# More filler transposes on TensorE in the first six pairs, written into idle columns of the score tile

## The chip, the cores and the metric

The kernel runs on one core of one Trainium2 chip. The metric is the device time of one execution in microseconds. Before the change it is 695.62 us, the median of three runs (695.5 to 698.72).

## What is computed

Attention over 8 batches of 8 heads, 576 positions and 64 features, with rotary positions on q and k, and then a gated feed-forward layer over the 512 features that the eight heads make together. Everything is in 32-bit floats. Cut to what matters:

```
q_rot, k_rot = rotate(q), rotate(k)
scores = q_rot @ k_rot.T / 8
scores = scores - max(scores, axis=-1)
attn = exp(scores);  attn = attn / (sum(attn, axis=-1) + 1e-9)
x = attn @ v                                   # heads side by side: (8, 576, 512)
gate = sigmoid(sum over 5 taps of conv_w[k] * x shifted by 4 - k rows)
out = ((gate * (x @ w_val)) @ w_out)
```

## The kernel before

**Pairs.** Two heads make a pair, so there are 32 pairs, four for each batch. A pair is worked through in five query chunks. Four of them have 128 queries for each of the two heads, the fifth, the odd chunk, holds the last 64 queries of both heads.

**A score step.** `s_mm` (L331) multiplies a chunk's queries with all 576 keys. It writes one score tile per head, two for a full chunk and one for the odd one. A score tile has two banks of PSUM, 2 x 512 columns, of which 2 x 288 are used. VectorE takes the maximum of each row (`s_max`, L337, tile `nm`), ScalarE the exp with the row sums (`s_exp`, L345, tile `p`). There are two score tiles in all (tags `ps_s0` and `ps_s1`), so the next chunk's scores can be written when the exps of this one have ended.

**What follows a step.** TensorE transposes the probabilities (L392, and L357 for the left-over columns) into a bank of another ring of four (tags `ps_t0` to `ps_t3`). ScalarE and VectorE copy them out (L430, L432), and TensorE multiplies them with v (L441, and L451 for the left-over rows) into such a bank. `x_norm` (L492) scales the result with the inverse sums, and the five taps and the gate follow on VectorE and ScalarE (L515 to L523).

**The feed-forward layer.** After every fourth pair, `f_mm` (L558) multiplies a batch's x with the two weights. Its matmuls stand between those of the pairs that follow. Its first ones here belong to batch 0 and stand behind pair 4's scores. Matmul operands are split into a high and a low part, and the weights are unpacked on VectorE (L594 to L606) during the first pairs.

**What sets the order.** A list written out by hand, `ORDER`, names the jobs one by one. Its position in that list is a job's step. Each engine does its jobs in that order. An entry's number after the colon is the ring slot that it takes. The tile framework adds the waits between engines: for every access to a tile it lets the instruction wait for the earlier accesses that it takes to be in conflict with it.

**Fillers.** The table `FILLS` gives some steps a number of transposes of the identity matrix that nobody reads, ahead of the step's job. Before the change there are 92 of them at nine steps, 32 at the very start. Each group takes a whole bank of the `ps_t` ring, whose slot the second number names:

```
def fill(n, slot):
    bank = psum.tile([128, 512], F32, name="ps_t", tag=f"ps_t{slot}")
    for _ in range(n):
        T.transpose(out=bank[:, 0:128], in_=ident, identity=ident)
```

Of the kernel before, what the change touches and what calls it, by code (L numbers as in the profile page):

```python
# [10 lines left out]
F32 = mybir.dt.float32  # L11
# [151 lines left out]
3271 3302:1 3272:1 3303 3273 3304 3274 3298 3305A:0 3299 3306 3312:3 3300A:2 3307:2 3301 3308 3309 3313 3310A:1 3317:1 3311 3318 3314 3319 3315V:0  # L163
3322:0 3320V:2 3323 3321 3324 3316 3325A:1 3326
"""
FILLS = {11: (32, 0), 17: (7, 1), 50: (19, 0), 63: (14, 2), 89: (7, 3), 101: (7, 0), 183: (2, 3), 287: (2, 1), 425: (2, 2)}


class Plan:
# [16 lines left out]
    def run(self, engine, fill):  # L186
# [6 lines left out]
        for step, entry in enumerate(ORDER.split()):  # L193
# [4 lines left out]
            writer.update(dict.fromkeys(w, i))  # L198
            if step in FILLS:
                fill(*FILLS[step])  # L200
            self.slots = [int(x) for x in slots]
# [5 lines left out]
def attn_gated_ffn(ctx: ExitStack, tc: tile.TileContext, q2, k2, v2, tab, w_val, conv_w, w_out, out, collect=None):  # L207
# [14 lines left out]
    V, A, G, T, SP = nc.vector, nc.scalar, nc.gpsimd, nc.tensor, nc.sync  # L222
# [5 lines left out]
    psum = ctx.enter_context(tc.tile_pool(name="psum", bufs=1, space=PSUM))  # L228
# [3 lines left out]
    def ring(tag, shape, dtype, name, where=pool):  # L232

        n = plan.slots.pop(0) if B[tag] > 1 else 0
        return where.tile(shape, dtype, name=name, tag=f"{tag}{n}")

    ident = const.tile([128, 128], F32, name="ident")
# [16 lines left out]
    state = {}  # L254
# [62 lines left out]
    def s_mm(p, c, second):  # L317

        st = state[p]
        heads = (0,) if c == 4 else (0, 1)  # L320
        tiles = []
        for h in heads:
            ps = ring("ps_s", [128, 2, 512], F32, "ps_s", psum)
            st[f"s{2 * c + h}"] = ps[:, :, 0:288]
            tiles.append(ps)
        for half in range(2):
            for i, (x, y) in enumerate(((0, 0), (0, 1), (1, 0))):
                for h in heads:
                    rows = slice(0, 128) if c == 4 else HEAD[h]
                    k0 = (0 if second else D) + half * 288  # L330
                    T.matmul(out=tiles[h][:, half, 0:288], lhsT=st["q"][rows, x, c * 128:c * 128 + 128],  # L331
                             rhs=st["k"][rows, y, k0:k0 + 288], start=(i == 0), stop=(i == 2))
# [14 lines left out]

    def fill(n, slot):

        bank = psum.tile([128, 512], F32, name="ps_t", tag=f"ps_t{slot}")  # L350
        for _ in range(n):
            T.transpose(out=bank[:, 0:128], in_=ident, identity=ident)  # L352

    def transpose(p, key, srcs):
        bank = ring("ps_t", [128, 512], F32, "ps_t", psum)
# [321 lines left out]
    for p in range(NP):  # L677
# [7 lines left out]
        for n in ("k", "q"):  # L685
            cut = 288 if n == "k" else 384
            for a, b in [(0, wide[n])] if p else [(0, cut), (cut, wide[n])]:
# [4 lines left out]
                if p < RAW:  # L692
                    add("GV", rope_mul, p, n, 1, a, b, r=tr + " " + x0, w=x1)
                    add("GV", rope_mul, p, n, 0, a, b, r=tr, w=x0)
                    for i, (x, y) in enumerate(((0, cut), (cut, wide[n]))):
                        if not a <= x < b:
                            continue
                        bank, hi, lo = f"ps_t/{n}{p}.{i}", f"{n}{par}#hi.{i}", f"{n}{par}#lo.{i}"
# [13 lines left out]
        for i, c in enumerate(order(p) + (4,)):  # L712
            r = kr + f" k{par}#w" * (i % 2) + " " + toks(f"q{par}#@.@", ("hi", "lo"), (0,) if c < 3 else R2)
            add("P", s_mm, p, c, i % 2, r=r, w=toks(f"ps_s/{p}.@", (2 * c, 2 * c + 1)[:1 + (c < 4)]))
            for x in (2 * c, 2 * c + 1)[:1 + (c < 4)]:
                t = f"{i // 2}{x % 2}" if c < 4 else "m"
                add("V", s_max, p, x, r=f"ps_s/{p}.{x}", w=f"nm/{p}.{x}")
                add("A", s_exp, p, x, t, i % 2, r=f"ps_s/{p}.{x} nm/{p}.{x}", w=f"p/{p}.{t}#{x} sums{par}#{x}")
# [87 lines left out]
    with tc.manual_schedule():  # L806
        plan.run({"V": V, "A": A, "G": G}, fill)
# [59 lines left out]
```

## Time and profile before

| | |
|---|---|
| runs | 698.72, 695.62, 695.5 us |
| the profiled execution | 699.4 us, span 697.5 us |
| mean granted clock of TensorE | 0.978 of full speed |
| TensorE busy | 669.6 us (96%), 7184 matmuls |
| VectorE busy | 585.9 us (84%) |
| ScalarE busy | 504.4 us (72%) |
| GpSimd busy | 308.1 us (44%) |
| the chain that ended last | TensorE 79%, VectorE 12%, ScalarE 6% |

Times are microseconds from the start of the span, and a matmul's durations overlap with the next one's: a busy TensorE is not TensorE at its peak. PE is TensorE's matmuls, PEld its weight loads, DVE VectorE, ACT ScalarE, POOL GpSimd. A row of the timeline gives the start, the length of the group, the engine, the line, and in brackets how long the engine was idle before it and what ended that. A row of groups gives the count, then busy time and mean ns of one, then the idle time before them and its releasers. A row of windows gives the stretch, and for PE, PEld, DVE, ACT and POOL the busy time with the count of instructions, then the granted clock, the share of the DMA engines and GB/s.

### The profile page before, as it was taken

What the parts mean: (1) busy time and instruction counts of PE and PEld (TensorE: products, weight loads), DVE (VectorE), ACT (ScalarE), POOL (GpSimd) and SP (SyncE); (2) the same over time, 40 slices, a digit from 0 to 9 for tenths busy, and PEclk for the clock granted to TensorE, in tenths of its full rate; (3) what the DMA queues carried; (4) which work ended last, traced back from release to release, by engine and by line L of the source; (5) the groups of instructions that cost most, each with busy time, mean ns of one, the idle gap of its engine ahead of it and who ended that gap; (6) DMA issues with size and microseconds to landing.
All of it is one profiled execution on the core that took longest, in us unless ns stands there. A gap on an engine that the chain in (4) does not pass through costs nothing.

```text
span 697.5 us, 18207 instructions
## 1 busy us (share of the span) xinstructions
PE 669.6 (96%) x7184; PEld 539.9 (77%) x7184; DVE 585.9 (84%) x1012; ACT 504.4 (72%) x1238; POOL 308.1 (44%) x236
## 2 busy tenths in 40 slices
PE   8888899899999999999999999999999999999998
PEld 7656567677778888787878888777788887788887
DVE  5998899999988868989899887998889889787741
ACT  3787877786877887778669877677678786777522
POOL 1344424264354765456334554366445553243031
PEclk9997769999999999999999999999999999999999
DMA  6344332433443143243432152433422144411011
GB/s 222 109 135 142 102 112 75 117 105 103 140 140 105 60 136 121 60 125 112 132 105 82 58 167 78 133 103 114 131 97 65 61 128 123 132 47 35 27 61 68
DMA packets 47318, 72.65 MB, mean 104 GB/s; under 512 B 15961, under 2 KB 25730, under 8 KB 47234
## 3 DMA queue, kind: packets, MB, share of 16 engines
q1 hardware_dynamic: 46690, 70.91, 32.8%
q8 instruction: 56, 0.92, 0.6%
q10 hardware_dynamic: 544, 0.59, 0.3%
q14 instruction: 28, 0.23, 0.1%
HBM read 61.89 MB, written 9.59 MB: 102 GB/s over the span
## 4 chain that ended last, share of the span: by engine, by line
PE 79%; DVE 12%; ACT 6%; issue 3%; POOL 0%; DVEq 0%; ACTq 0%; POOLq 0%
PE ps_f L558 27%; PE ps_s L331 18%; PE ps_a L441 17%; PE ps_t L392 10%; DVE nm L337 4%; ACT p L345 3%; PE ps_a L451 3%; PE ps_t L357 2%; DVE g L518 2%; ACT pt L430 2%; PE ps_t L352 1%; DVE q L303 1%; DVE pt L432 1%; PE ps_r L286 1%; ACT q L295 0%
## 5 line engine op out<-in xcount | busy, mean ns | idle before, releaser
L345 ACT ACTIVATE p<-ps_s,nm 128x576 f32<-128x576 f32 x288 | 212.7, 742 | 70.7 <-DVE nm L337 68.5
L337 DVE TENSOR_REDUCE nm<-ps_s 128x1 f32<-128x576 f32 x288 | 207.9, 750 | 44.7 <-PE ps_s L331 40.4
L331 PE MATMUL ps_s<-k,q 64*128 64x288 f32 (+1 forms) x1728 | 184.4, 315 | 14.6 <-ACT p L345 14.0
L331 PEld LDWEIGHTS ps_s<-k,q 64*128 64x128 f32 (+1 forms) x1728 | 143.6, 190 | 48.0 <-ACT p L345 33.7
L430 ACT COPY pt<-ps_t 128x512 f32<-128x512 f32 (+1 forms) x228 | 120.9, 547 | 54.8 <-PE ps_t L392 52.9
L441 PE MATMUL ps_a<-pt,v 128*64 128x256 f32 (+1 forms) x1024 | 139.9, 416 | 1.2 <-DVE pr L432 0.7
L518 DVE SCALAR_TENSOR_TENSOR g<-x,cw,g 128x576 f32<-128x576 f32 (+1 forms) x132 | 121.0, 918 | 1.4 <-ACT g L515 0.9
L392 PEld LDWEIGHTS ps_t<-ident,p 64*128 64x128 f32 x2428 | 101.5, 141 | 22.4 <-issue 9.6
L392 PE MATMUL ps_t<-ident,p 64*128 64x64 f32 x2428 | 113.4, 229 | 3.9 <-ACT p L345 1.3
L558 PE MATMUL ps_f<-y,wout_hi 128*128 128x288 f32 (+2 forms) x512 | 107.4, 302 | 0.7 <-DVE pt L432 0.5
L441 PEld LDWEIGHTS ps_a<-pt,v 128*64 128x64 f32 x1024 | 68.8, 138 | 46.9 <-issue 3.8
L573 POOL TENSOR_TENSOR y<-y,y 128x288 fp32r<-128x288 f32 (+2 forms) x64 | 57.2, 905 | 105.0 <-ACT y L570 101.6
L558 PEld LDWEIGHTS ps_f<-y,wout_hi 128*128 128x128 f32 x512 | 81.4, 188 | 6.4 <-issue 1.5
L275 POOL TENSOR_TENSOR qin<-qin,tab 128x640 f32<-128x640 f32 (+1 forms) x36 | 58.2, 1627 | 55.1 <-DMA qin<-in_q 44.0
L558 PE MATMUL ps_f<-xh,wval_hi 128*128 128x288 f32 (+2 forms) x256 | 79.1, 313 | 1.1 <-ACT pt L430 1.1
L558 PE MATMUL ps_f<-xh,wval_lo 128*128 128x288 f32 (+2 forms) x256 | 76.4, 301 | 0.0
L558 PE MATMUL ps_f<-xl,wval_hi 128*128 128x288 f32 (+2 forms) x256 | 75.5, 298 | 0.0
L558 PE MATMUL ps_f<-y,wout_lo 128*128 128x288 f32 (+2 forms) x256 | 74.4, 294 | 0.0
L275 POOL TENSOR_TENSOR kin<-kin,tab 128x576 f32<-128x576 f32 x27 | 43.7, 1625 | 62.7 <-DMA kin<-in_k 52.1
L505 POOL TENSOR_TENSOR xl<-x,xh 128x576 fp32r<-128x576 f32 (+2 forms) x33 | 48.2, 1463 | 50.6 <-ACT xh L499 31.1
L432 DVE COPY pt<-ps_t 128x512 f32<-128x512 f32 (+1 forms) x92 | 56.8, 623 | 5.3 <-PE ps_t L392 4.7
L345 ACT ACTIVATION_READ_ACCUMULATOR p<-ps_s,nm 128x1 f32 x288 | 57.3, 199 | 0.0
(87 smaller groups left out, 860.9 us busy)
## 6 DMA issues: line engine op xcount, KB each, us to landing
kin<-in_k SPq DMA_DIRECT2D x31, 576.0 KB
qin<-in_q SPq DMA_DIRECT2D x31, 512.0 KB
v<-in_v SPq DMA_DIRECT2D x32, 320.0 KB
out_t<-o SPq DMA_DIRECT2D x56, 144.0 KB
rb<-rd SPq DMA_DIRECT2D x31, 144.0 KB
rb<-rd SPq DMA_DIRECT2D x31, 128.0 KB
wst<-in_w_val SPq DMA_DIRECT2D x4, 512.0 KB
wst<-in_w_out SPq DMA_DIRECT2D x8, 256.0 KB
```

What stands on the lines that cost most here:

```text
L275: eng.tensor_tensor(out=t[:, i, a:b], in0=t[:, 0 if p < RAW else i, a:b], in1=table[:, i, a:b], op=ALU.mult)
L331: T.matmul(out=tiles[h][:, half, 0:288], lhsT=st["q"][rows, x, c * 128:c * 128 + 128], rhs=st["k"][rows, y, k0:k0 + 288], start=(i == 0), ...
L337: V.tensor_reduce(out=st[f"nm{i}"], in_=st[f"s{i}"], axis=AX.XY, op=ALU.max, negate=True)
L345: A.activation(out=st[f"p{t}"][:, part].rearrange("p (b x) -> p b x", b=2), in_=st[f"s{i}"], func=AF.Exp, bias=st[f"nm{i}"], scale=1.0, ac ...
L392: T.transpose(out=st["b" + key + x][:, k * D:(k + 1) * D], in_=src[rows], identity=ident[rows, rows])
L430: A.copy(out=dst, in_=src)
L432: V.tensor_copy(out=dst, in_=src)
L441: T.matmul(out=st[f"a{g}"][HEAD[h], 0:n], lhsT=st["v"][:, j, h, :], rhs=st[f"pt{g}"][:, h * 4 + j], start=(j == 0), stop=False)
L505: G.tensor_tensor(out=st["xl"][:, a:b], in0=xs[p % 2][:, 4 + a:4 + b], in1=st["xh"][:, a:b].bitcast(F32), op=ALU.subtract)
L518: V.scalar_tensor_tensor(out=g, in0=x_sb[:, a + k:b + k], scalar=w, in1=g, op0=ALU.mult, op1=ALU.add)
L558: T.matmul(out=acc[:, 0:n], lhsT=wt[w][:, kc, ds], rhs=mv, start=(kc == 0 and i == 0), stop=(kc == NCH - 1 and i == 2))
L573: G.tensor_tensor(out=ffn[b][1][:, dc, lo:hi], in0=ffn[b, "y", dc, lo], in1=ffn[b][0][:, dc, lo:hi].bitcast(F32), op=ALU.subtract)
```

## The change

The table has 28 steps in the place of nine, and 242 transposes in the place of 92. The steps lie between 11 and 614 of 3,327, in pairs 0 to 5. All but the two groups at steps 11 and 17 have the slot -1. That sends them to the score tile that was allocated last, into columns 384 to 511 of its second half, which `s_mm` doesn't write. They no longer take a bank of the `ps_t` ring.

```
-FILLS = {11: (32, 0), 17: (7, 1), 50: (19, 0), 63: (14, 2), 89: (7, 3), 101: (7, 0), 183: (2, 3), 287: (2, 1), 425: (2, 2)}
+FILLS = {11: (32, 0), 17: (8, 1), 50: (19, -1), 63: (14, -1), 77: (11, -1), 89: (8, -1), 101: (8, -1), 145: (4, -1), 164: (8, -1), 176: (4, -1), 183: (3, -1),
+         191: (8, -1), 253: (24, -1), 263: (3, -1), 278: (5, -1), 287: (3, -1), 350: (15, -1), 364: (14, -1), 375: (10, -1), 387: (6, -1), 400: (3,
+         -1), 425: (2, -1), 451: (2, -1), 458: (6, -1), 487: (3, -1), 557: (9, -1), 573: (3, -1), 614: (7, -1)}
...
             st[f"s{2 * c + h}"] = ps[:, :, 0:288]
+            state["score"] = ps
...
-        bank = psum.tile([128, 512], F32, name="ps_t", tag=f"ps_t{slot}")
+        if slot < 0:
+            to = state["score"][:, 1, 384:512]
+        else:
+            to = psum.tile([128, 512], F32, name="ps_t", tag=f"ps_t{slot}")[:, 0:128]
         for _ in range(n):
-            T.transpose(out=bank[:, 0:128], in_=ident, identity=ident)
+            T.transpose(out=to, in_=ident, identity=ident)
```

The order on VectorE, ScalarE, GpSimd and the DMA queue is the same as before. TensorE's order differs by the fillers alone. Two places of it follow. In the rows, `[waits ...]` names the engines whose semaphores the instruction waits for, and the six new lines of code move the line numbers: L334 is the old L331, L358 the old L352, L398 the old L392 and L363 the old L357.

TensorE before, pair 0, from the end of the first score step to the transposes behind the second:

```order
L331 MATMUL ps_s<-k_71,q_73 128x288 x7
L352 MATMUL ps_t<-ident 128x128 x19
L331 MATMUL ps_s<-k_71,q_73 128x288 [waits Activation_49] x2
L331 MATMUL ps_s<-k_71,q_73 128x288 x10
L392 MATMUL ps_t<-ident,p 128x64 [waits PE_49]
L392 MATMUL ps_t<-ident,p 128x64 x15
```

The same place after the change:

```order
L334 MATMUL ps_s<-k_71,q_73 128x288 x7
L358 MATMUL ps_s<-ident 128x128 [waits Activation_49]
L358 MATMUL ps_s<-ident 128x128 x18
L334 MATMUL ps_s<-k_71,q_73 128x288 [waits PE_49] x2
L334 MATMUL ps_s<-k_71,q_73 128x288 x10
L398 MATMUL ps_t<-ident,p 128x64 x16
```

The 19 fillers had no wait. Now the first of them waits for ScalarE, for the exp of the score tile that they write into. The wait of the next two score matmuls for ScalarE is gone; they wait for TensorE's own earlier work, the second of them for the fillers.

TensorE before, pair 2, ahead of the fourth full chunk and of the odd chunk (the last row):

```order
L392 MATMUL ps_t<-ident,p 128x64 x14
L331 MATMUL ps_s<-k_71,q_73 128x288 [waits Activation_49]
L331 MATMUL ps_s<-k_71,q_73 128x288 [waits PE_49,Activation_49]
L331 MATMUL ps_s<-k_71,q_73 128x288 x10
L392 MATMUL ps_t<-ident,p 128x64 [waits PE_49]
L392 MATMUL ps_t<-ident,p 128x64 [waits Activation_49]
L392 MATMUL ps_t<-ident,p 128x64 x14
L357 MATMUL ps_t<-ident,p 128x128 [waits DVE_49]
L357 MATMUL ps_t<-ident,p 128x128
L331 MATMUL ps_s<-k_71,q_73 128x288 [waits Activation_49]
```

The same place after the change:

```order
L398 MATMUL ps_t<-ident,p 128x64 x14
L358 MATMUL ps_s<-ident 128x128 [waits Activation_49]
L358 MATMUL ps_s<-ident 128x128 x23
L334 MATMUL ps_s<-k_71,q_73 128x288 [waits PE_49] x2
L334 MATMUL ps_s<-k_71,q_73 128x288 x10
L398 MATMUL ps_t<-ident,p 128x64
L398 MATMUL ps_t<-ident,p 128x64 [waits Activation_49]
L398 MATMUL ps_t<-ident,p 128x64 x14
L358 MATMUL ps_s<-ident 128x128 [waits DVE_49]
L358 MATMUL ps_s<-ident 128x128 x2
L363 MATMUL ps_t<-ident,p 128x128 x2
L334 MATMUL ps_s<-k_71,q_73 128x288 [waits Activation_49]
```

24 fillers stand ahead of the fourth chunk and wait for the exp of the third. Three stand ahead of the left-over transposes and wait for VectorE, for the maximum of the fourth.

## The prediction

> **What bounds the kernel now.** I read the page first, then the windows of three long stretches, then the timeline of one score step, then the groups of the score lines, and last the windows cut along the changes of the granted clock.
>
> The page's busy shares over the span, and the granted clock in 40 slices:
>
> ```profile
> PE 669.6 (96%) x7184; PEld 539.9 (77%) x7184; DVE 585.9 (84%) x1012; ACT 504.4 (72%) x1238; POOL 308.1 (44%) x236
> PEclk9997769999999999999999999999999999999999
> ```
>
> ```profile
> 0.00:115.00 115.00, 99.97 (x951) 74.61 (x953) 99.83 (x189) 81.27 (x200) 40.76 (x35) 0.87 0.41 131
> 115.00:150.00 35.00, 32.20 (x353) 24.51 (x353) 33.99 (x71) 27.29 (x71) 12.84 (x13) 1.00 0.43 127
> 150.00:697.50 547.50, 537.43 (x5888) 440.76 (x5885) 452.06 (x754) 395.85 (x969) 254.50 (x189) 1.00 0.32 97
> ```
>
> After 150 us TensorE is busy 537.4 of 547.5 us: whatever happens before it moves that stretch as a whole, one for one. The change lies before it. There TensorE is idle 15 us of 115, and its clock is 0.87 on average. So the question is what a score step consists of in the first pairs. The first steps of pair 0 in the timeline:
>
> ```profile
> 12.87 1.17 PE L331 MATMUL ps_s<-k,q 64*128 64x288 f32 x12
> 13.97 2.29 PE L352 MATMUL ps_t<-ident 128*128 128x128 f32 x19
> 14.37 1.42 DVE L337 TENSOR_REDUCE nm<-ps_s 128x1 f32<-128x576 f32 x2
> 15.88 0.73 ACT L345 ACTIVATE p<-ps_s,nm 128x576 f32<-128x576 f32 x1
> 16.50 0.20 ACT L345 ACTIVATION_READ_ACCUMULATOR p<-ps_s,nm 128x1 f32 x1
> 16.76 0.93 PE L331 MATMUL ps_s<-k,q 64*128 64x288 f32 x10 [0.17 <-ACT p L345]
> 18.25 1.42 DVE L337 TENSOR_REDUCE nm<-ps_s 128x1 f32<-128x576 f32 x2
> 18.25 1.75 PE L352 MATMUL ps_t<-ident 128*128 128x128 f32 x14
> ```
>
> This is a ring. Score matmuls (L331), two maxima (L337), two exps (L345), and only when the second exp ends (16.50 + 0.20 = 16.70) do the next score matmuls go on (16.76), because there are two score tiles. TensorE's 19 old fillers fit into that wait. How tight the ring is, the groups tell, for 12.6 to 57 us (first two rows) and for 57 to 116 us:
>
> ```profile
> L331 PE MATMUL ps_s<-k,q 64*128 64x288 f32 (+1 forms) x135 | 16.1, 317 | 3.5 <-ACT p L345 3.4
> L337 DVE TENSOR_REDUCE nm<-ps_s 128x1 f32<-128x576 f32 x22 | 15.7, 751 | 0.9 <-PE ps_s L331 0.8
> ...
> L331 PE MATMUL ps_s<-k,q 64*128 64x288 f32 (+1 forms) x149 | 22.2, 379 | 7.7 <-ACT p L345 7.6
> L337 DVE TENSOR_REDUCE nm<-ps_s 128x1 f32<-128x576 f32 x24 | 17.4, 753 | 5.2 <-PE ps_s L331 5.1
> ```
>
> VectorE waits for scores only 0.9 us in the first stretch, since it has other work up to the moment they arrive, but it has hardly any to spare: a score step that comes later leaves it idle. In the second stretch it already waits 5.2 us. That is where the clock is low. These windows are cut at the clock's own changes (columns: busy us of PE, PEld, DVE, ACT, POOL, then the granted clock):
>
> ```profile
> 46.71:50.13 3.41, 2.35 (x42) 1.86 (x40) 3.38 (x8) 3.23 (x11) 0.00 (x0) 1.00 0.55 169
> ...
> 56.95:60.37 3.41, 1.92 (x28) 1.57 (x28) 3.41 (x6) 2.01 (x5) 1.65 (x1) 1.00 0.52 176
> 60.37:63.78 3.41, 2.30 (x26) 2.30 (x27) 2.66 (x6) 2.05 (x5) 1.77 (x2) 0.50 0.12 26
> ...
> 80.85:84.26 3.41, 1.88 (x33) 1.52 (x31) 3.32 (x6) 3.20 (x7) 1.32 (x1) 1.00 0.51 172
> ...
> 104.74:108.15 3.41, 2.34 (x28) 1.67 (x26) 3.41 (x8) 2.15 (x6) 3.16 (x2) 1.00 0.33 115
> 108.15:111.56 3.41, 3.41 (x16) 3.41 (x15) 3.27 (x9) 2.86 (x7) 1.27 (x2) 0.50 0.00 0
> ```
>
> Each slow spell follows a window in which TensorE was busy 1.9 to 2.3 of 3.41 us. A window of 2.35 did not bring one, so the bound is near there. The spells begin at 60.4, 84.3 and 108.2; by the mean clock of 0.87 they last (1 - 0.87) x 115 / 0.5 = 30 us in all.
>
> **The change part by part.** It adds 150 transposes (242 for 92), moves the fillers from a transpose bank to the newest score tile, and changes nothing in the other engines' order. First the price of one, from the groups of 2 to 5 us and of 6.2 to 6.9 us and from a matmul behind them:
>
> ```profile
> L352 PE MATMUL ps_t<-ident 128*128 128x128 f32 x16 | 3.6, 417 | 0.0
> L352 PE MATMUL ps_t<-ident 128*128 128x128 f32 x9 | 1.1, 273 | 0.0
> 7.52 0.72 PE L286 MATMUL ps_r<-kin,ident 128*128 128x288 f32 x2 [0.33 <-PE ps_t L352]
> ```
>
> They overlap. At full clock the 14 at 18.25 take (1.75 - 0.27) / 13 = 0.11 us each; at half clock (3.6 - 0.42) / 15 = 0.21. A matmul that must wait until the last one has landed loses some 0.2 us more: the last starts 0.11 before the next could, lands after 0.27, and the release takes about 0.05.
>
> The second thing is where they stand in time, and this decides. The order rows shown with the change give each group a wait that it did not have: for ScalarE (or VectorE), and the score matmuls behind it now wait for the group. In the program the value waited for is the exp that reads the very tile into which the group writes; the idle columns don't count. But that exp is the one whose end also ends TensorE's wait. So the group does not run in the gap. It starts when the gap is over (16.76 in the step above), and the next scores come later by its whole length. The gap itself stays empty, including those that the old fillers filled.
>
> I sum what this adds per score step: group length plus 0.2, less what the maximum behind it had to spare.
>
> - *Pairs 0 and 1* (12.9 to 57 us). On the ring stand 19, 14, 11, 4 and 8, also 8 behind pair 0's odd chunk that hold up attention matmuls and then the next scores, and 8 that hold up the transposes after pair 1's odd chunk: 72 x 0.11 = 7.9, plus 0.2 for five of them = 8.9. To spare: 0.5 at 18.25 (the scores end at 17.7), about 0.1 at the others: some 0.8 in all. Covered are the 8 before the odd chunk of pair 0, whose scores end at 27.78 while the maximum starts at 28.95, because VectorE is busy elsewhere, and in the same way 4 + 3 in pair 1. Without that cover they would cost another 1.6. Sum **+8.1**.
>
> ```profile
> 26.72 1.06 PE L331 MATMUL ps_s<-k,q 128*128 128x288 f32 x6 [0.25 <-ACT p L345]
> 28.95 0.76 DVE L337 TENSOR_REDUCE nm<-ps_s 128x1 f32<-128x576 f32 x1
> ...
> 57.71 0.77 PE L392 MATMUL ps_t<-ident,p 64*128 64x64 f32 x16
> 61.48 1.80 PE L331 MATMUL ps_s<-k,q 64*128 64x288 f32 x11 [1.44 <-ACT p L345]
> 63.09 0.76 DVE L337 TENSOR_REDUCE nm<-ps_s 128x1 f32<-128x576 f32 x1 [0.75 <-PE ps_s L331]
> 66.61 0.76 DVE L337 TENSOR_REDUCE nm<-ps_s 128x1 f32<-128x576 f32 x1 [1.37 <-PE ps_s L331]
> 75.98 1.42 DVE L337 TENSOR_REDUCE nm<-ps_s 128x1 f32<-128x576 f32 x2 [1.75 <-PE ps_s L331]
> 83.44 1.15 PE L331 MATMUL ps_s<-k,q 64*128 64x288 f32 x11 [0.32 <-ACT p L345]
> 85.24 1.42 DVE L337 TENSOR_REDUCE nm<-ps_s 128x1 f32<-128x576 f32 x2
> 86.91 1.81 PE L331 MATMUL ps_s<-k,q 128*128 128x288 f32 x6 [1.47 <-ACT p L345]
> 107.55 1.35 PE L331 MATMUL ps_s<-k,q 128*128 128x288 f32 x6 [0.82 <-ACT p L345]
> 127.73 0.44 PE L357 MATMUL ps_t<-ident,p 128*128 128x128 f32 x2 [0.89 <-DVE x L492]
> 130.32 0.71 PE L392 MATMUL ps_t<-ident,p 64*128 64x64 f32 x15 [0.58 <-ACT pt L430]
> 137.84 0.40 PE L558 MATMUL ps_f<-xh,wval_hi 128*128 128x288 f32 x1 [1.09 <-ACT pt L430]
> ```
>
> - *Pair 2's large gap.* 24 transposes start at 61.48 and take 2.6 + 0.2. At full clock the scores then need 1.05 instead of 1.8, so +2.1. The 3 and 5 behind are paid by the faster matmuls (VectorE's 1.37 of waiting at 66.61). The attention matmuls before 75.98 give back the 1.75: together **+0.4** if the clock stays up.
> - *Pair 3 and pair 4's start* (82 to 98 us): 15, 14, 10, then 6 and 3. 15 is 1.8, less 0.65 to spare (scores done at 84.59, maximum at 85.24); the others 1.7 and 1.3, less about 0.8 each from scores at full clock; the last two about even with the second spell's slow attention matmuls. **+2.3** with the clock up.
> - *From 98 us on.* 2 and 6 are hidden in the 0.82 before 107.55, 3 and 7 in waits of 0.6 and 1.1 after 130 us. Three stand before pair 5's first scores (+0.6). Nine must wait for an exp that ends 0.3 after 127.73 and then take 1.0 (+1.4). The third spell is 3.41 us at half clock, 1.7 of work; I let it give back 1.3, since the next maximum also waits for an exp. **+0.7**.
>
> With the clock up throughout the sum is 8.1 + 0.4 + 2.3 + 0.7 = **+11.5 us**. The other end is the same spells as before: the 68 transposes in them take 0.10 more each (+7.0), and the 5.2 us of VectorE's waiting and the 1.3 of the third spell are not given back: 11.5 + 7.0 + 6.5 = **+25 us**.
>
> Which of the two? The gaps are still empty, so windows below 2.3 will occur. The wait before 61.48 begins at 58.5 and stays 3 us; the one from 14.0 to 16.76, filled until now, opens too, and a spell there would cost 19 x 0.10 + 0.75 = 2.7. Against that, each large gap is now followed by a dense run: 24 transposes and the scores are about 7 us at half clock, in which a whole fully busy window fits, and after such a one (108.15, busy 3.41) the clock came back. I take one short spell at the first score step or at pair 2's gap, about 3 us, and nothing else: **+14.5**.
>
> Does such a run of transposes lift the clock at all? The rows say yes: between the 417 ns at 2 to 5 us and the 273 ns at 6.2 us nothing but transposes had run on TensorE (the clock column shows 1.00 there because its record begins later; the durations tell). [...]
>
> The profiled execution took 699.4 us with a span of 697.5; the runs' median is 695.62, so I carry the difference: 695.6 + 14.5 = **710**.
>
> **The rivals.**
>
> *The slow spells stay, and the transposes run at half clock*: 695.6 + 25 = 721. For it: the gaps stay empty. Against it: the dense run after each. [...] Chance 0.2.
>
> *The gaps do get filled and the spells vanish* (the other side): then VectorE's 5.2 us of waiting in the second stretch are the most that can be won, as it works on through the rest: 695.6 - 5 = 690.5. For it: three spells follow three thin windows. It decides if the exp waited for has ended by the time TensorE arrives, so that the group starts at 58.5 rather than at 61.48. Against it: at 61.48 and at 86.91 the score matmuls themselves were released by an exp. Chance 0.05.
>
> *The added work drowns in VectorE's*: it is busy 99.8 of the first 115 us, and if the later scores met a VectorE that was behind anyway, 695 to 698 would come out. It would need more to spare than the 0.1 to 0.4 between the scores' end and the maximum. Chance 0.05.
>
> **How the numbers follow.** My case, late scores with the clock mostly up, has 0.70, and 702 to 717 as its own range: the low end if only half of the added lengths reach the end, the high end with two or three spells. With the second case the range is 702 to 721. The two small cases lie below it. A measurement of this kernel tells about 0.5% (3.5 us) from no change: faster 0.05, within it 0.05, slower 0.90.
>
> **What would show it.** Right: the new transposes of pair 2 start after the exp at about 61.5 plus the earlier delay, not before; VectorE's waiting for scores in the first 130 us grows from 6 to some 20 us; the stretch after pair 5 is as long as before. Wrong: fillers that start right behind the transposes of the probabilities; a clock of 1.00 with VectorE's waiting below 6 us; or a clock near 0.97 with 720.

## The result, and the profile after

The changed kernel is slower: 718.07 us median (715.69 to 720.8) against 696.43 for the kernel before beside it, a ratio of 1.031, 95% interval 1.026 to 1.036. That is +21.6 us, where the prediction had +14.5 (710, range 702 to 721). The profiled execution took 719.58 us with a span of 717.7; before it was 699.4 and 697.5.

From the page of the changed kernel, busy shares and granted clock:

```profile
PE 682.0 (95%) x7334; PEld 553.8 (77%) x7334; DVE 583.6 (81%) x1012; ACT 505.3 (70%) x1238; POOL 307.8 (43%) x236
PEclk9999889999999999999999999999999999999999
```

The 150 extra transposes are there (7334 matmuls for 7184), TensorE's busy time grew by 12 us, and the clock's mean went up, from 0.978 to 0.987. VectorE and ScalarE do the same work as before and the time still grew by 20 us in the profile, so the rows have to show which waits grew. The same place as in the prediction, pair 0 behind the first score step (timeline, old L331 is L334, L337 is L340, L345 is L348, L352 is L358):

```profile
14.66 1.42 DVE L340 TENSOR_REDUCE nm<-ps_s 128x1 f32<-128x576 f32 x2
16.18 0.73 ACT L348 ACTIVATE p<-ps_s,nm 128x576 f32<-128x576 f32 x1
16.80 0.20 ACT L348 ACTIVATION_READ_ACCUMULATOR p<-ps_s,nm 128x1 f32 x1
17.05 3.84 PE L358 MATMUL ps_s<-ident 128*128 128x128 f32 x19 [2.71 <-ACT p L348]
...
20.82 1.18 PE L334 MATMUL ps_s<-k,q 64*128 64x288 f32 x12
...
21.92 1.42 DVE L340 TENSOR_REDUCE nm<-ps_s 128x1 f32<-128x576 f32 x2 [2.86 <-PE ps_s L334]
```

The old 19 fillers started at 13.97, in the gap. The new ones start at 17.05, behind the second exp's end at 17.00, and TensorE stood idle for 2.71 us before them. The next scores wait until 20.82 (16.76 before), and VectorE, which had not waited there at all, waits 2.86. Groups over the first 115 us of before and, for the same work, the first 135 us of the changed kernel:

```profile
L337 DVE TENSOR_REDUCE nm<-ps_s 128x1 f32<-128x576 f32 x45 | 32.3, 752 | 6.1 <-PE ps_s L331 5.8
```

```profile
L340 DVE TENSOR_REDUCE nm<-ps_s 128x1 f32<-128x576 f32 x45 | 32.4, 753 | 24.3 <-PE ps_s L334 23.5 <-PE ps_s L358 0.5
L334 PE MATMUL ps_s<-k,q 64*128 64x288 f32 (+1 forms) x282 | 31.2, 321 | 0.3
L358 PE MATMUL ps_s<-ident 128*128 128x128 f32 x183 | 30.3, 320 | 23.1 <-ACT p L348 20.8 <-DVE nm L340 2.3
```

VectorE's wait for scores went from 6.1 to 24.3 us. The score matmuls themselves no longer wait (0.3 us); the fillers ahead of them do, 23.1 us, 20.8 of it for an exp. The gaps were not filled. They moved ahead of the fillers.

How far the work is behind by then, at a later score step (the 45th, pair 8's odd chunk), before and changed:

```profile
194.49 0.76 DVE L337 TENSOR_REDUCE nm<-ps_s 128x1 f32<-128x576 f32 x1 [0.29 <-PE ps_s L331]
```

```profile
216.90 0.76 DVE L340 TENSOR_REDUCE nm<-ps_s 128x1 f32<-128x576 f32 x1 [0.30 <-PE ps_s L334]
```

It is 22.4 us late there and 20.2 at the end. Everything was lost in the first pairs, as the prediction said. The clock in the changed kernel, cut at its own changes (columns as before: PE, PEld, DVE, ACT, POOL, granted clock):

```profile
13.44:16.85 3.41, 0.90 (x12) 0.58 (x10) 3.34 (x7) 1.62 (x5) 1.20 (x1) 1.00 0.98 375
16.85:20.27 3.42, 3.22 (x15) 3.22 (x16) 2.13 (x6) 0.77 (x3) 0.20 (x1) 0.50 0.28 97
...
68.10:71.50 3.40, 1.51 (x27) 1.37 (x27) 3.34 (x6) 2.00 (x5) 1.65 (x1) 0.99 0.51 175
71.50:74.90 3.40, 2.29 (x11) 2.30 (x12) 1.96 (x4) 2.05 (x5) 1.76 (x2) 0.50 0.13 16
74.90:78.30 3.40, 3.40 (x17) 3.07 (x17) 0.00 (x0) 0.00 (x0) 2.30 (x2) 0.50 0.78 263
78.30:81.70 3.40, 2.11 (x34) 1.98 (x34) 2.15 (x4) 1.45 (x4) 0.00 (x0) 1.00 0.24 92
95.40:98.80 3.40, 1.45 (x20) 1.31 (x17) 3.40 (x6) 3.32 (x8) 1.07 (x2) 1.00 0.42 137
98.80:102.20 3.40, 3.40 (x30) 3.07 (x30) 1.01 (x2) 0.90 (x2) 1.99 (x1) 0.50 0.00 0
102.20:105.60 3.40, 1.27 (x19) 1.13 (x16) 2.81 (x5) 2.04 (x5) 0.00 (x0) 1.00 0.00 0
105.60:109.00 3.40, 3.40 (x22) 3.12 (x22) 0.29 (x1) 0.36 (x1) 0.00 (x0) 0.50 0.00 0
```

Four slow spells, 17 us in all, in the place of one that was forecast. Each follows a window in which TensorE, waiting ahead of a filler group, was busy 0.90 to 1.51 us. Each ends after a window that is nearly full (3.22 to 3.40 us), and each of these full windows holds a large group, the last two only a part of one beside score matmuls.

### The profile page after: what moved, and what is told of

It reads as the page before. It is cut to its first block, busy times and chain, and to the rows that moved or that the text cites. A ratio compares the mean times of both kernels' runs of the same rounds, so it can differ in the third digit from the quotient of the medians.

```text
span 717.7 us, 18503 instructions
## 1 busy us (share of the span) xinstructions
PE 682.0 (95%) x7334; PEld 553.8 (77%) x7334; DVE 583.6 (81%) x1012; ACT 505.3 (70%) x1238; POOL 307.8 (43%) x236
## 4 chain that ended last, share of the span: by engine, by line
PE 81%; DVE 9%; ACT 5%; issue 2%; DMA 1%; SPq 0%; POOL 0%; DVEq 0%; ACTq 0%; POOLq 0%
PE ps_f L564 27%; PE ps_s L334 19%; PE ps_a L447 15%; PE ps_t L398 10%; PE ps_s L358 4%; ACT p L348 4%; DVE nm L340 4%; PE ps_a L457 3%; PE ps_t L363 2%; DVE g L524 2%; PE ps_t L358 1%; DMA qin<-in_q 1%; DVE q L305 1%; ACT pt L436 1%; PE ps_r L288 1%
## 5 line engine op out<-in xcount | busy, mean ns | idle before, releaser
L348 ACT ACTIVATE p<-ps_s,nm 128x576 f32<-128x576 f32 x288 | 212.9, 743 | 84.7 <-DVE nm L340 81.7
L340 DVE TENSOR_REDUCE nm<-ps_s 128x1 f32<-128x576 f32 x288 | 208.0, 751 | 65.9 <-PE ps_s L334 61.2
L334 PE MATMUL ps_s<-k,q 64*128 64x288 f32 (+1 forms) x1728 | 178.6, 311 | 4.7 <-ACT p L348 3.6
L334 PEld LDWEIGHTS ps_s<-k,q 64*128 64x128 f32 (+1 forms) x1728 | 140.0, 187 | 36.5 <-ACT p L348 18.8
L447 PE MATMUL ps_a<-pt,v 128*64 128x256 f32 (+1 forms) x1024 | 137.8, 412 | 0.2 <-ACT pt L436 0.2
L524 DVE SCALAR_TENSOR_TENSOR g<-x,cw,g 128x576 f32<-128x576 f32 (+1 forms) x132 | 119.3, 906 | 1.6 <-ACT g L521 1.0
L398 PEld LDWEIGHTS ps_t<-ident,p 64*128 64x128 f32 x2428 | 99.1, 139 | 18.2 <-issue 8.9
L398 PE MATMUL ps_t<-ident,p 64*128 64x64 f32 x2428 | 110.5, 226 | 0.4 <-ACT p L348 0.2
L348 ACT ACTIVATION_READ_ACCUMULATOR p<-ps_s,nm 128x1 f32 x288 | 57.3, 199 | 0.0
```

The source lines that it names most:

```text
L340: V.tensor_reduce(out=st[f"nm{i}"], in_=st[f"s{i}"], axis=AX.XY, op=ALU.max, negate=True)
L348: A.activation(out=st[f"p{t}"][:, part].rearrange("p (b x) -> p b x", b=2), in_=st[f"s{i}"], func=AF.Exp, bias=st[f"nm{i}"], scale=1.0, ac ...
L398: T.transpose(out=st["b" + key + x][:, k * D:(k + 1) * D], in_=src[rows], identity=ident[rows, rows])
L447: T.matmul(out=st[f"a{g}"][HEAD[h], 0:n], lhsT=st["v"][:, j, h, :], rhs=st[f"pt{g}"][:, h * 4 + j], start=(j == 0), stop=False)
L524: V.scalar_tensor_tensor(out=g, in0=x_sb[:, a + k:b + k], scalar=w, in1=g, op0=ALU.mult, op1=ALU.add)
```

## The experiments

The theory going in: a group in the newest score tile waits for the exp that reads this tile, starts when the gap is over, and delays the next scores by its length; the rest is slow clock. Its rivals: the waits don't matter and it is the number or the length of the fillers; or the clock does not matter. All experiments compute the whole output; they differ in fillers alone.

**The same fillers without that wait.** 228 transposes at 26 of the 28 steps (145 and 375 left out), in free `ps_t` banks:

```
-FILLS = {..., 50: (19, -1), 63: (14, -1), 77: (11, -1), 89: (8, -1), 101: (8, -1), ...}
+FILLS = {..., 50: (19, 0), 63: (14, 2), 77: (11, 1), 89: (8, 3), 101: (8, 0), ...}
```

> The change's own steps and counts, but each group writes into a bank of the transpose ring whose last copy is over, not into the score tile; the two groups (4 and 10 transposes) for which no such bank is free are left out, so 228 transposes in place of 242. Theory (the wait for the score tile's exp is what costs): the groups run inside the gaps, VectorE's waiting for scores falls back to some 6 us before 130 us, the clock stays up nearly throughout, and the time is 689 to 697 us. Rival (the added transposes cost as work, wherever they stand): 136 more than before at 0.11 us are 15 us and the time is 708 to 716 us.

Measured 700.41 us, a ratio of 1.003 (1.001 to 1.005), clock 0.998 to 1.00. The number of transposes is not what costs 21 us. VectorE's wait for scores is back at 6.9 us over the first 117 us (6.1 before). The theory's own time was missed too: the clock was won, and still the kernel was no faster. Its longest groups outlast the gap, or wait for something themselves:

```profile
24.00 1.42 PE L358 MATMUL ps_t<-ident 128*128 128x128 f32 x11 [0.98 <-DVE pt L438]
...
62.65 2.84 PE L358 MATMUL ps_t<-ident 128*128 128x128 f32 x24 [1.63 <-ACT pt L436]
```

The 11 wait for VectorE's copy out of their bank and made the next maximum 1.15 us later than before, the 24 made it 0.9 later.

**The old nine steps, moved to the score tile.** No more fillers than before; only the place is changed:

```
+FILLS = {11: (32, 0), 17: (7, 1), 50: (19, -1), 63: (14, -1), 89: (7, -1), 101: (7, -1), 183: (2, -1), 287: (2, -1), 425: (2, -1)}
```

> The nine steps and 92 transposes of before, but the seven groups inside the pairs write into the newest score tile. Theory: 19, 14 and 7 come onto the score ring (2.1 + 1.5 + 0.8, plus 0.2 each, less 0.5 to spare), 7 before the odd chunk are covered, the opened gap at 14 us brings a slow spell of 2 to 3 us: 5 to 8 us more than before, 701 to 705 us. Rival (only the number of transposes counts): no change, 695 to 698 us.

704.59 us, 1.010 (1.008 to 1.012): seven groups with 53 transposes cost 7 us by their place alone. The theory's number came out, its parts less well. In the trace the first six score steps lose 8.4 us, with two slow spells (from 22.5 and 32.8 us) and none at 14, and the 7 ahead of the odd chunk, put down as covered, come with 1.7 of it. By the 45th step 3.6 us of the 8.4 are given back, mostly where the kernel before has its own spells.

**No fillers in the gaps at all.**

```
+FILLS = {11: (32, 0), 17: (7, 1)}
```

> Only the two groups ahead of the first scores (32 and 7) stay; no transposes that nobody reads inside the pairs. Theory: fillers in gaps cost nothing and buy some clock, so without them the gap at 14 to 16.7 us brings a slow spell early and the time is that of before plus 0 to 4 us: 696 to 701 us. Rival (fillers cost as work): 53 fewer at 0.11 us, 690 to 692 us.

701.74 us, 1.006 (1.005 to 1.008), clock 0.966 to 0.978. The rival is refuted: the old fillers weren't costing anything. The theory's range was missed by 0.7 us. The old fillers are worth some 4 us, and the old nine steps in the new place (704.6) are worse than none.

**The same fillers in the other score tile**, that of the pair's first head, whose exp ends first:

```
-            state["score"] = ps
+            state["score"] = tiles[0] if tiles else ps
```

> The change as it is, but the groups write into the older of the two score tiles of a step. Nothing else differs, and the count is the same 242. Theory: most groups may start when the first exp has ended, 0.7 us before the second (1.8 us at the 24 of pair 2), so some ten groups on the ring cost 0.7 us less each: 708 to 714 us. Rival (the count decides): 716 to 720 us as with the newest tile.

708.63 us, 1.016 (1.013 to 1.019), clock 0.998 to 1.00, and within the theory's range. Half of the loss goes away, partly by the clock, when the exp waited for is the earlier one of the two. Pair 2's 24 show it:

```profile
65.00 0.74 ACT L348 ACTIVATE p<-ps_s,nm 128x576 f32<-128x576 f32 x1 [1.40 <-DVE nm L340]
65.64 0.19 ACT L348 ACTIVATION_READ_ACCUMULATOR p<-ps_s,nm 128x1 f32 x1
...
66.84 0.74 ACT L348 ACTIVATE p<-ps_s,nm 128x576 f32<-128x576 f32 x1
...
65.89 2.84 PE L358 MATMUL ps_s<-ident 128*128 128x128 f32 x24 [1.15 <-ACT p L348]
68.78 1.06 PE L334 MATMUL ps_s<-k,q 64*128 64x288 f32 x12
```

The 24 start right behind the first exp (65.83) and run under the second one, so this score step added 0.55 us to the delay. In the changed kernel it added 4.95, and 2.4 in the kernel with four gaps filled (below), at full clock. With this the wait and its target are settled. What remained was the size.

**One transpose per group** at the same 26 steps, so that the waits stay and the length goes; and **half of each group**:

```
+FILLS = {11: (32, 0), 17: (8, 1), 50: (1, -1), 63: (1, -1), 77: (1, -1), ...}     # one_each
+FILLS = {11: (32, 0), 17: (8, 1), 50: (10, -1), 63: (7, -1), 77: (6, -1), ...}    # half_each
```

> The changed kernel with one transpose in the place of 2 to 24 in each of the 26 groups in the score tile: the waits stay, the length goes. Theory (a group costs 0.2 us for its wait plus 0.11 us for each transpose): some 14 groups on the ring cost 0.3 us each, 4 us, on top of the kernel with no fillers in the gaps, whose slow spells it shares: 704 to 707. Rival (the wait itself is the price, whatever the length): 714 to 718, as the changed kernel.

> The changed kernel with each of the 26 groups in the score tile cut to half, 107 transposes for 202. Theory (cost by length): of the 11.5 us with the clock up some 5 go away, and two to four slow spells stay, 8 us with their worth: 708 to 713. Rival (waits alone): 715 to 718.

712.95 us, 1.023 (1.021 to 1.026), and 713.93, 1.024 (1.021 to 1.027). The first misses the theory by 6 us, the second by 1. 26 single transposes cost nearly as much as 107 (16.5 and 17.5 us) and three quarters of what 202 cost. At the 45th step the profiled executions are 11.8, 15.4 and 22.4 us late, more clearly in the order of the lengths. But the clock was quite different. With one each, over the first 135 us and in the longest of three slow spells:

```profile
0.00:135.00 135.00, 111.48 (x1016) 82.19 (x1016) 109.59 (x207) 87.29 (x216) 43.84 (x38) 0.80 0.37 120
...
15.90:39.80 23.90, 18.72 (x148) 14.56 (x150) 16.88 (x33) 12.80 (x33) 5.54 (x4) 0.50 0.27 90
```

The spells last 23.9, 13.7 and 17.1 us, 55 of the first 108. Either the wait itself is dear, or the emptied gaps cost through the clock and the longer groups pay part of that back.

**One transpose per group, with the gaps filled.** Ahead of 20 of these groups, 130 transposes go into free banks (the expectations say 117, but the table adds up to 130), and wait for nothing that the gap waits for:

```
+GAPS = {50: (19, 0), 63: (14, 2), 89: (8, 3), 101: (7, 0), 164: (6, 0), 176: (2, 3), ...}
...
+            if step in GAPS:
+                fill(*GAPS[step])
             if step in FILLS:
```

> The kernel with one transpose per group in the score tile, which took 713 with slow clock in 55 of its first 108 us, and ahead of 20 of these groups the 117 transposes in free banks, which keep the clock up. Theory (a wait by itself costs 0.2 to 0.3 us for each of some 14 groups on the ring, and the rest of 713 was clock): clock above 0.995, and 4 us over the kernel with the fitted bank fillers alone, 699 to 702. Rival (the wait costs more than the length, clock or not): 709 to 713.

701.34 us, 1.006 (1.004 to 1.008), clock 0.995 to 1.00. 130 more transposes made the kernel 11.6 us faster, by the clock. What is left over the fitted bank fillers alone (696.46, below; the same 130) is 4.9 us for 26 single transposes and their waits, where 4 were expected; the two profiled executions are 6.6 apart. The rival is refuted. At the 45th step:

```profile
196.67 0.76 DVE L341 TENSOR_REDUCE nm<-ps_s 128x1 f32<-128x576 f32 x1 [0.28 <-PE ps_s L335]
```

```profile
206.26 0.76 DVE L338 TENSOR_REDUCE nm<-ps_s 128x1 f32<-128x576 f32 x1 [0.30 <-PE ps_s L332]
```

The first is the filled kernel, the second that with one each alone: 9.6 us apart.

**The changed kernel with the gaps filled**, in the same way at 20 steps, and at only the four whose gaps were followed by a slow spell:

```
+GAPS = {50: (19, 0), 63: (14, 2), 89: (8, 3), 101: (7, 0), 164: (6, 0), ...}   # both_fills
+GAPS = {50: (19, 0), 253: (14, 3), 350: (15, 1), 364: (14, 2)}                 # four_gaps
```

> The changed kernel, and ahead of 20 of its groups as many transposes in a free transpose bank as the gap holds (2 to 19, 117 in all), which wait for nothing that the gap waits for. So the gaps are filled and the clock stays up, and the groups in the score tile still hold up the next scores. Theory (the part of the loss beyond the forecast is slow clock): clock above 0.995, and the sum of the prediction with the clock up, 11.5 us: 706 to 711. Rival (the delays are longer than the prediction's prices, clock or not): 715 to 719 with the clock above 0.995.

> The changed kernel, with 62 transposes in free transpose banks ahead of only those four groups whose empty gaps were followed by a slow spell (19, 14, 15, 14, at steps 50, 253, 350, 364). Theory (the loss beyond the forecast is slow clock: the four score steps came 1.5, 2.5, 1.3 and 1.5 us later than in the kernel with both kinds of fillers at full clock): clock above 0.996 and some 6 us less than the changed kernel's 718, 710 to 714. Rival (the delays of the waits are the whole loss, and the kernel with both kinds of fillers was no faster for that reason): 716 to 719 with the clock above 0.996.

With all 20: 718.05 us, 1.030 (1.026 to 1.033), with the clock at 0.999. By time this is the rival's number, not the theory's. The groups in banks themselves delay three score steps by 3.3 us more than the kernel with four gaps filled has there. At the 45th step the kernel is 19.4 us late (first maximum at 213.88). Without the 3.3 that is 16.1, larger than the 11.5 of the prediction, but 6.3 less than the changed kernel's 22.4.

With four: the profiled execution took 712.06 us with the clock at 1.00, and at the 45th step it is 6.75 us ahead of the changed kernel (216.90), which is what the four spells were expected to be worth:

```profile
0.00:135.00 135.00, 115.30 (x1206) 89.90 (x1208) 107.15 (x203) 86.80 (x215) 43.96 (x38) 1.00 0.36 116
```

```profile
210.15 0.76 DVE L343 TENSOR_REDUCE nm<-ps_s 128x1 f32<-128x576 f32 x1 [0.29 <-PE ps_s L337]
```

But its other four executions had a clock of 0.994 to 0.998 and took 716.2 to 718.1. The median is 716.25, 1.028 (1.024 to 1.032), which can't be told from the changed kernel. So the worth of the spells is shown by score steps, in two traces: at the four steps behind these gaps the changed kernel loses 6.9 us more than this one, and as much more than the one with all 20 gaps filled. The times neither bear it out nor refute it.

**The changed kernel without its largest group**, the 24 at step 253:

> The changed kernel without its largest group, the 24 ahead of pair 2's fourth chunk, which stood in a slow spell and came with 4.95 us of the loss. Theory A (its length is what it costs): 712 to 714. Theory B (24 transposes in a row are also what brings the clock back; without them the spell goes on until the next dense stretch, as it does with one transpose per group): the slow spell that begins near 71 us lasts 10 us or more in the place of 6.8, and the time is 715 to 718.

718.94 us, 1.032 (1.028 to 1.035): no faster, and a little above theory B's range. B's spell is there: it went on for twice as long, 13.7 us. The score step behind the gap added nothing to the delay in the place of 4.95 us, and the steps behind it paid only a part: over steps 14 to 18 the delay grew by 1.22 us in the place of 3.07. At the 45th step this kernel is 3.6 us ahead of the changed one (213.30 for 216.90), and it loses most of that again by the end (spans of 717.1 and 717.7), where no filler differs. So the trace shows that the 24 bring the clock back, but the time doesn't show that their length is paid for by that. First the 24 in the changed kernel, then the spell without them:

```profile
72.61 5.38 PE L358 MATMUL ps_s<-ident 128*128 128x128 f32 x24 [3.00 <-ACT p L348]
77.92 1.28 PE L334 MATMUL ps_s<-k,q 64*128 64x288 f32 x12
```

```profile
70.80:84.50 13.70, 10.91 (x79) 9.33 (x81) 8.95 (x18) 8.52 (x20) 5.62 (x4) 0.50 0.29 92
```

**Bank fillers fitted to the gaps.** As the first experiment, without four of its groups (steps 77, 451, 458, 557) and with no group longer than its gap:

```
-FILLS = {..., 77: (11, 1), 191: (8, 2), 253: (24, 3), 278: (5, 1), 387: (6, 2), 451: (2, 1), 458: (6, 1), 557: (9, 0), ...}
+FILLS = {..., 191: (2, 2), 253: (14, 3), 278: (2, 1), 387: (4, 2), ...}
```

> As the kernel with all 28 fillers in free transpose banks, but no group is longer than the wait it stands in: 24 become 14, 8 become 2 before the odd chunk of pair 1, 11, 2, 6 and 9 are left out where there was no wait to fill. That kernel took 1.0031 of before's time with the clock at 1.00 throughout, and its score steps came 1.15, 0.45, 0.23, 0.27, 0.91 and 1.19 us later at just these groups. Theory (fillers without a wait, no longer than the gap, cost nothing, and the clock's gain of 4 to 5 us stays): 1.0031 less some 4 us, 694 to 697, clock 1.00. Rival (the longer groups were what held the clock, and a slow spell comes back): clock below 0.995 and 698 to 702.

696.46 us, 0.9995 (0.997 to 1.002), clock 0.993 to 1.00. No version here beats the kernel before. At the 45th step it is 4.5 us ahead of the profiled execution of before:

```profile
190.00 0.76 DVE L338 TENSOR_REDUCE nm<-ps_s 128x1 f32<-128x576 f32 x1 [0.30 <-PE ps_s L332]
```

That execution (699.4, clock 0.978) was one of the slower ones of before, though; most have a clock of 0.985 to 0.990 and 695 to 697 us, with less to win. And the twelve executions of the fitted kernel lie between 693.0 and 700.8 with a clock near 1.00 throughout. What moves them by some 4 us either way isn't settled. It need not lie in the first pairs. Between the 45th step and the end, where no filler differs, the traces change their delay by anything from -3.5 us (the other tile) to +3.0 (no fillers in the gaps). A difference of some 3 us between two of these times can come from there.

## Why the direction was right and the size short

**The mechanism held.** The new groups start behind the exp; pair 2's 24 start at 72.61 (61.5 plus the delay of 11.1), not in the gap. VectorE's wait for scores grew to 24.3 us, where about 20 was forecast. The seven moved groups, the other tile and the single transposes all go by this wait. The stretch behind passes the delay on, less 2.2 of 22.4 us. The rival with gaps filled and the one in which the work drowns are out.

The number, though, has luck in it. My own case ended at 717, and the measured 718.07 lies in the range only because the upper rival had widened it to 721.

**The size was short by 7.9 us** at the 45th step (22.4 for 14.5). For the terms I took the start of the first maximum of each of these 45 score steps, less its start before, and added up the growth by stretch. The kernel with four gaps filled serves as the changed kernel at full clock:

```
                                   predicted,    four_gaps    changed     changed less
                                   clock up      (clock 1.00)  kernel      four_gaps: spells
pairs 0 and 1 (to step 13)           +8.1          +9.71        +11.13       +1.42
pair 2's gap (steps 14 to 18)        +0.4          +0.56         +3.07       +2.51
pair 3, pair 4's start (19 to 22)    +2.3          +3.53         +6.38       +2.85
from there on (23 to 45)             +0.7          +1.86         +1.83       -0.03
sum                                 +11.5         +15.66        +22.41       +6.75
slow spells                          +3                                      +6.75
```

- *The clock, mis-sized by some 3.7.* "One short spell at the first score step or at pair 2's gap, about 3 us, and nothing else." There was one at both, and two more in pair 3. A row that pointed to these was in the prediction: in the kernel before, the window from 80.85, with the open gap ahead of pair 3's fourth chunk, was busy 1.88 us and brought a spell. I counted spells at two gaps and let pair 3's pass, though the change leaves them open too; the windows there were busy 1.45 and 1.27 us. Much of a spell's price is the groups themselves: the 19 took 3.84 us for 2.29 at full clock, the 24 took 5.38 for 2.84.
- *The bound of 2.3 us* that I read off for these windows does not hold. In the changed kernel the window from 78.30 was busy 2.11 us and brought no spell, and in the trace of before one from 135.46, which the prediction leaves out, was busy 2.23 and brought none either. In all thirteen traces, cut on each one's own grid of 3.41 us from 8 us on, the 15 windows at full clock that were busy 0.83 to 1.55 us were all followed by half clock. From 1.67 (four gaps filled, at 21.18) to 2.34 some were and most were not, so the busy time alone doesn't decide there.
- *The cover, 1.0.* I took the 8 ahead of pair 0's odd chunk and the groups in pair 1 as hidden by a busy VectorE, and named 1.6 us without that. They cost 0.43, 0.20 and 0.42 at full clock.
- *The odd chunk, 0.8.* I priced every wait at 0.2. But an odd chunk's scores need only the tile of the first head, and their fillers write into that of the second. So the scores, too, now wait for the second exp. Pair 3's odd chunk, first with the fitted bank fillers, then with a single transpose in the score tile:

```profile
83.90 0.19 ACT L346 ACTIVATION_READ_ACCUMULATOR p<-ps_s,nm 128x1 f32 x1
...
84.62 0.20 ACT L346 ACTIVATION_READ_ACCUMULATOR p<-ps_s,nm 128x1 f32 x1
...
84.29 1.03 PE L332 MATMUL ps_s<-k,q 128*128 128x288 f32 x6
```

```profile
87.58 0.19 ACT L349 ACTIVATION_READ_ACCUMULATOR p<-ps_s,nm 128x1 f32 x1
...
88.29 0.20 ACT L349 ACTIVATION_READ_ACCUMULATOR p<-ps_s,nm 128x1 f32 x1
...
88.55 0.33 PE L359 MATMUL ps_s<-ident 128*128 128x128 f32 x1 [0.34 <-ACT p L349]
88.63 1.04 PE L335 MATMUL ps_s<-k,q 128*128 128x288 f32 x6
```

  The scores start 0.20 us behind the first exp's end in the one and 0.14 behind the second's in the other. The step with 14 transposes was put at +0.9; it came to +1.7.
- *A collision, 1.2*, which no filler causes (last section), and about 1.1 in small differences, 0.4 of it at the very first maximum. Some 0.25 is a slip: the terms for pair 3 (1.8 less 0.65, 1.7 and 1.3 less 0.8 each) add up to 2.55, not to 2.3.

One more step: the prediction took the difference between two traces and added it to a median. The profiled executions are 20.2 us apart, the medians 21.6, and the profiled execution of before was one of its slower ones.

The price of one transpose was right. Between the kernel with one each and gaps filled and the one with four gaps filled, the second score step grew from -0.13 to +1.84 with 18 more transposes: 0.11 us each.

**The transposes do lift the clock.** In the window from 74.90 to 78.30 TensorE ran transposes until 77.99, and the clock was full behind it; without the 24 the spell lasted 13.7 us instead of 6.8. The time came near the upper rival's 721, but by short spells and longer delays, not by the old long spells.

## What to carry to other kernels

A filler belongs into memory whose last reader has long finished, since the wait that the framework adds goes with the tile and not with the columns; else it starts when the gap is over. Ask for every such write which instruction reads the tile last, and whether the work behind was waiting for that one or for an earlier one. A gap that is left open can cost twice, once as a wait and once as half clock in the windows behind it; here the second was 11.6 of 16.5 us with single transposes.

## What the runs showed of the hardware

**Half clock comes and goes in windows of 3.41 us.** The spells of all kernels here last 3.4, 6.8, 10.2, 13.7, 17.1 or 23.9 us, in steps of 3.41. The executions of one kernel differ in clock (0.983 to 0.990 for the changed one), and no run shows why. In the traces the grid lies differently against the start of the span: taken modulo 3.41 us, the first spell starts at 3.2 in the changed kernel (16.85), at 2.3 in the one before (60.37) and at 2.0 in the one with the old nine steps moved (22.5). A drop doesn't need an idle window: it followed windows in which TensorE was busy for 0.90 to 1.51 of 3.41 us in the changed kernel, and for 1.88 to 2.34 in the one before. Windows of about 2 us can also pass: one of 2.11 did in the changed kernel.

**Where a tap on VectorE meets a `kin` instruction on GpSimd, the later one takes longer.** The step whose first maximum starts at 143.49 us before adds 1.2 us to the delay in the changed kernel, and as much in the kernel with the fitted bank fillers, which has no filler in the score tile at all. It is the profiled execution of before that escaped it: of the other twelve traces all but the one with half of each group (0.03) add 0.9 to 1.3 us at this step. The rows of VectorE and GpSimd, before and changed:

```profile
142.43 0.81 DVE L518 SCALAR_TENSOR_TENSOR g<-x,cw,g 128x576 f32<-128x576 f32 x1
...
142.53 2.32 POOL L275 TENSOR_TENSOR kin<-kin,tab 128x576 f32<-128x576 f32 x1 [2.71 <-DVE wst L596]
```

```profile
163.66 1.98 DVE L524 SCALAR_TENSOR_TENSOR g<-x,cw,g 128x576 f32<-128x576 f32 x1
...
163.46 1.57 POOL L277 TENSOR_TENSOR kin<-kin,tab 128x576 f32<-128x576 f32 x1 [2.42 <-DMA kin<-in_k]
```

In these rows the one that starts first takes 0.81 us (VectorE) or 1.57 (GpSimd), and when it comes second VectorE's takes 1.17 us longer and GpSimd's 0.75. Before, VectorE was 0.10 us ahead; now GpSimd is 0.20 ahead, and the ring pays. With four gaps filled GpSimd is 0.16 us ahead and with the fitted bank fillers 0.11, and VectorE's instruction takes 1.98 us in both. A shift of 0.3 us between the two engines so cost 1.2 us here, which no sum of waits foresees.
